# Interleaving the channels of a fused convolution and soft-MoE kernel, storing four evictions at a time, and giving the planner later landings

## The chip, the cores and the metric

The kernel runs on one core of a Trainium2 chip. The metric is the device time of one execution in microseconds, as the median of several runs; a run's time is a little longer than the span that the profiler draws from the first to the last instruction. The engines are named as in the profile: PE (matmul; PEld is its weight load), DVE (vector), ACT (scalar), POOL (GpSimd) and SP, which here only issues DMAs.

## The reference

The first half is a convolution whose seven taps are drawn anew for every token and head and go through a softmax; the second half is a soft mixture of experts over its output. Cut to what matters:

```python
B, S, D, H, K = 8, 3584, 192, 8, 7              # group = D // H = 24 channels per head
w = softmax(weight_gen, axis=-1)                # [B, S, H, K]
x_unf[b, s, k] = x_pad[b, s + k]                # the last 7 tokens
x = einsum('bshk,bskhg->bshg', w, x_unf).reshape(B * S, D)      # 28672 tokens

logits = x @ phi                                # [28672, 32]: 8 experts x 4 slots
d = softmax(logits, axis=0)                     # over the tokens, per slot
slot_in = d.T @ x                               # [32, 192]
slot_out[e] = relu(slot_in[e] @ w1[e]) @ w2[e]  # per expert, hidden width 1024
c = softmax(logits, axis=1)                     # over the slots, per token
out = c @ slot_out                              # [28672, 192]
```

Everything is float32.

## The kernel before

**Tiling.** Tokens are cut into blocks of T = 26 (with the six before them 32 rows), four blocks make a group, and there are 276 groups; two groups make a pair (138 pairs), four pairs a block of the loop, eight pairs a unit (17 units, and a last one of two pairs). One softmax chunk of taps serves eight groups, that is one block of the loop. `x` lies in `big` as block diagonal by head, so that one matmul with a 128x26 weight (four heads by 32 rows; `band`, the taps laid out as a band matrix) and 96 moving columns (four heads by 24 channels) gives the convolution of one block for four heads. A float32 matmul shows up as two MATMUL records in the trace.

**The stages.**

- *The loop.* For each pair, `conv` makes 16 matmuls into one PSUM bank (`cv`), four at a time in the four 32-row quadrants of the output, and ACT copies the 384 columns into `tm` (`conv_out`). In a pair's row of `tm` stand, between two ones, the 192 channels of the even group and the 192 of the odd group. `xpose` turns three pieces of 128 columns per pair by PE transposes, and ACT copies them into `cm`. The middle piece holds 64 channels of the even and 64 of the odd group; the odd group's halves are swapped, so that it ends with its first 96 channels.
- *Logits, per unit.* `logits` multiplies `cm` with `phi`: for each of the two groups of a pair and each of the two pieces that the group touches, four matmuls (one per quadrant) of 8 pairs x 26 = 208 columns. DVE takes the maximum (`top`, row L288, then L290), PE spreads it over the partitions (`newmax`, L306), DVE reduces it again (L310), ACT takes the exponential (L318), DVE transposes it (L327) and PE adds the tokens to the slots (`dispatch`, L346), two units being in flight.
- *The tail of the loop and the experts.* After the last rescale of the slot sums `accS` (L354), PE sums the even and odd groups' sums into slot inputs (`pst`, L704 to L706, and `psu`); the odd selector `selO4` and the zeros of `si` are made on POOL (L689, L690). Then come the expert matmuls (L742, L763).
- *The output.* For each of 16 steps of 17 or 18 groups, `rows` multiplies the transposed token weights `cT` with the slot outputs; ACT and DVE copy PSUM to `big` (`leave`, L823: an *eviction* of two PSUM banks), and SP stores it (`store`, L830). `out_order` lists 24 *items*; an item is four quarters of a step, in two evictions. The first item is stored in three parts, the second in two, every other whole. `big` is a ring of 16 eviction slots.

**What sets the order.** In the loop every step is an entry `op(engine, cost, reads, writes, function, ..., late=..)` of a list. PE's and SP's entries keep the list's order. For DVE, ACT and POOL a planner (`model`) plays the list with the costs given, a DMA's result being there `cost + late` after its issue begins, and lets each engine take the ready entry with the least slack; the sort by the times that it finds is the order in the program. On the chip every engine then works through its instructions strictly in that order, so a DVE instruction that waits for a DMA holds up all that stand behind it. The taps of a chunk are loaded by `loadw` (L160) and first read by `tap_top` (L171) on DVE; `tap_sub` (L175) follows on POOL, an exponential on ACT, a sum on POOL, a reciprocal on DVE (L194), a product on POOL (L202), and the transpose into the band on DVE (L206).

The two entries whose numbers matter:

```python
op(SP, 0.4, [], [("w", c % NTAP, b) for b in range(CH)], loadw, c, late=4.0)
op(SP, 2.0, [("z", i, h) for h in range(4)], [x_of(i)], loadx, i, late=3.0)
```

Of the kernel before, what the change touches and what calls it, by code (L numbers as in the profile page):

```python
# [8 lines left out]
F32 = mybir.dt.float32  # L9
# [41 lines left out]
def conv_soft_moe(ctx, tc, xh, wh, phi, w1a, w1b, w2, out):  # L51
# [169 lines left out]
    def conv(p):  # L221
        cv = cvs[p % NCV]
        for par in range(2):
            g = 2 * p + par
            t = g // SGG
            for c in range(2):
                for blk in range(4):
                    o = 4 * GW * (2 * par + (c ^ par))
                    i, b = ((4 * (g % m) + blk) * 2 + c for m in (4, SGG))
                    P.matmul(cv[32 * blk : 32 * blk + T, o : o + 4 * GW],  # L230
# [43 lines left out]
    def logits(u, lo=0, hi=UP):  # L274
        hi = min(hi, UNITS[u][1])
        cm = cms[u]
        lp = lss(u).rearrange("p (a b) j -> p a b j", b=2)
        for par in range(2):
            for i in range(2):
                for blk in range(4):  # L280
                    P.matmul(lp[32 * blk : 32 * blk + 32, lo:hi, par, 0:T],  # L281
                             phi_sb[:, 2 * par + i, :], cm[:, lo:hi, 1 if i else 2 * par, blk, :],
                             start=(i == 0), stop=(i == 1))
# [261 lines left out]
    for k in range(BLOCKS):  # L545
# [11 lines left out]
        for c in range(NTAP, NCH):  # L557
            if k == max(0, c - 4):
                op(SP, 0.4, [], [("w", c % NTAP, b) for b in range(CH)], loadw, c, late=4.0)
        for t in range(NSG):  # L560
            if (SGG * t + SGG - 1) // (2 * Q) == k:
                if t + NXS < NSG:
                    for i in (NXS - 1, NXS) if t == 0 else (t + NXS,):
                        op(SP, 2.0, [("z", i, h) for h in range(4)], [x_of(i)], loadx, i, late=3.0)
# [28 lines left out]
    op(PO, 0.3, [], tmf, drop, final)  # L593
    op(TE, 0.21 * FILL[0], [], [("cv", (PAIRS + 1) % NCV)], fill, FILL[0])
    op(TE, 0.19 * n, cm_of(final), [("ls", 1), spare], logits, final)
# [93 lines left out]
    G.tensor_tensor(out=selO4, in0=sel4, in1=selE4, op=ALU.subtract)  # L689
    G.memset(si, 0.0)  # L690
# [14 lines left out]
    P.matmul(pst[0:96], accS[:, 96:192], sO, start=False, stop=True)  # L705
    P.matmul(pst[96:128], accS[:, 0:32], sO, start=False, stop=True)  # L706
# [5 lines left out]
    for r in (0, 64):  # L712
        P.matmul(psu[r : r + 64], accS[:, 129 : D + 1], sE, start=True, stop=False)
        P.matmul(psu[r : r + 64], accS[:, 32:96], sO, start=False, stop=True)
# [121 lines left out]
    for kind, h, stores in out_order():  # L836
        for parts in stores:
            slot += -slot % len(parts)
            lo = at = slot % OT * 2 * 18 * T
            for qs in parts:  # L840
                po = ps_o.tile([128, 2, 512], F32, tag="po", name=f"po{kind}{h}_{qs[0]}")
                for i, q in enumerate(qs):
                    if kind == 0:
# [102 lines left out]
```

## Time and profile before

| | us |
|---|---|
| three runs | 307.57, 302.77, 307.64 |
| median of the runs | 307.57 |
| the profiled execution's own time | 305.91 |
| its span | 304.1 |
| first convolution matmul to the last rescale of the slot sums | 13.55 to 228.30 |
| experts, up to the first output matmul | to 244.52 |
| output: first store issued, last bytes moved | 246.23, 302 |

PE is busy for 263.5 us (87%) of the span, DVE for 197.2 (65%), ACT for 189.6 (62%), POOL for 146.6 (48%). These shares average over a loop in which PE hardly rests and an output stage in which the DMA engines do not, so they are read stage by stage. Lines marked L are lines of the kernel before; in the changed kernel most move by one.

### The profile page before, as it was taken

The page shows a single profiled execution, that of the slowest core. Times are in us where ns is not written, and L with a number is a line of the kernel's source. Part 1 is how long each engine was busy: PE and PEld are TensorE (multiplying, and loading weights), DVE is VectorE, ACT ScalarE, POOL GpSimd, SP SyncE. Part 2 cuts the span into 40 slices and gives each one's busy share as a digit, 9 for nine tenths or more (in the row PEclk, how much of TensorE's full clock was granted, in tenths as well). Part 3 has the DMA queues.
Part 4 walks back from the last instruction along what each step waited for, and adds up shares of the span by engine and source line. Part 5 has one row for each costly group of instructions (what it writes and reads, how often), then busy time and mean ns, then how long its engine had stood idle before and what let it go on. Part 6 is the DMA issues. An engine that isn't in the chain of part 4 may idle for free.

```text
span 304.1 us, 15222 instructions
## 1 busy us (share of the span) xinstructions
PE 263.5 (87%) x6646; PEld 213.7 (70%) x6646; DVE 197.2 (65%) x337; ACT 189.6 (62%) x399; POOL 146.6 (48%) x254
## 2 busy tenths in 40 slices
PE   8898998999999999999999999499899887889100
PEld 8787977888897888888988889488678632233000
DVE  8867757975787867775776855554056579995200
ACT  9896676576686767677767667255521268788400
POOL 8856556746468384665565463410017526550000
PEclk9999999999999999999999999979999999779855
DMA  6768676667677667666677666626748059999994
GB/s 184 220 180 240 201 214 199 208 205 207 185 216 202 201 187 202 195 194 193 185 222 216 188 204 195 195 81 182 255 130 314 3 202 416 421 410 417 419 418 204
DMA packets 26993, 69.24 MB, mean 228 GB/s; under 512 B 5936, under 2 KB 10800, under 8 KB 26928
## 3 DMA queue, kind: packets, MB, share of 16 engines
q1 hardware_dynamic: 26928, 68.28, 69.0%
q8 instruction: 52, 0.85, 1.2%
q14 instruction: 13, 0.11, 0.1%
HBM read 46.21 MB, written 22.04 MB: 224 GB/s over the span
## 4 chain that ended last, share of the span: by engine, by line
PE 69%; DMA 9%; DVE 7%; issue 4%; ACT 3%; POOL 3%; ACTq 1%; POOLq 0%; DVEq 0%
PE cv L230 30%; PE pt L250 14%; PE acb L346 7%; PE ls L281 7%; DMA out<-big 4%; DMA taps<-wh 4%; PE po L818 3%; PE so L763 2%; PE hpb L742 2%; PE acb L306 2%; DVE big L823 1%; DVE band L206 1%; POOL taps L175 1%; ACT big L823 1%; DVE cT L404 1%
## 5 line engine op out<-in xcount | busy, mean ns | idle before, releaser
L230 PE MATMUL cv<-big,band 128*26 128x96 f32 x4416 | 112.3, 250 | 3.6 <-issue 2.6
L230 PEld LDWEIGHTS cv<-big,band 128*26 128x26 f32 x4416 | 101.5, 130 | 13.0 <-issue 8.1
L236 ACT COPY tm<-cv 128x384 f32<-128x384 f32 x138 | 66.4, 482 | 57.6 <-PE cv L230 57.4
L206 DVE STREAM_TRANSPOSE band<-wide 128x1664 f32<-128x1664 f32 (+1 forms) x37 | 65.5, 1773 | 7.8 <-POOL wide L202 7.6
L250 PE MATMUL pt<-ident,tm 122*128 122x122 f32 x414 | 50.9, 272 | 0.2 <-issue 0.2
L257 ACT COPY cm<-pt 128x416 f32<-128x416 f32 x103 | 48.1, 511 | 1.9 <-PE pt L250 0.9
L250 PEld LDWEIGHTS pt<-ident,tm 122*128 122x128 f32 x414 | 44.5, 144 | 2.6 <-issue 0.4
L202 POOL TENSOR_TENSOR wide<-exps,sum 128x364 f32<-128x364 f32 (+1 forms) x36 | 28.5, 792 | 26.5 <-DVE sum L194 18.9
L175 POOL TENSOR_TENSOR taps<-taps,top 128x364 f32<-128x364 f32 (+1 forms) x36 | 28.5, 793 | 24.3 <-DVE top L171 24.0
L818 PE MATMUL po<-cT,so 32*128 32x442 f32 (+3 forms) x256 | 33.6, 629 | 5.4 <-ACT big L823 3.4
L823 ACT COPY big<-po 128x884 f32<-128x884 f32 (+2 forms) x33 | 28.1, 893 | 7.8 <-PE po L818 6.0
L818 PEld LDWEIGHTS po<-cT,so 32*128 32x128 f32 (+1 forms) x256 | 12.1, 171 | 26.4 <-ACT big L823 18.0
L188 POOL TENSOR_TENSOR si<-exps 128x208 f32<-128x208 f32 x32 | 20.3, 635 | 21.0 <-ACT exps L179 20.6
L281 PE MATMUL ls<-cm,phi_sb 128*32 128x208 f32 x544 | 28.9, 338 | 1.5 <-issue 1.5
L171 DVE TENSOR_REDUCE top<-taps 128x52 f32<-128x364 f32 (+1 forms) x37 | 17.7, 486 | 18.4 <-DMA taps<-wh 17.7
L346 PE MATMUL acb<-tm,dt 128*32 128x193 f32 x544 | 27.5, 328 | 2.3 <-issue 1.6
L87 POOL TENSOR_TENSOR LT<-LT,rm 128x544 f32<-128x544 f32 (+1 forms) x16 | 17.9, 1120 | 16.8 <-DVE rm L85 16.8
L288 DVE TENSOR_REDUCE mx<-ls 128x1 f32<-128x416 f32 x17 | 9.9, 584 | 24.0 <-PE ls L281 24.0
L281 PEld LDWEIGHTS ls<-cm,phi_sb 128*32 128x32 f32 x544 | 17.8, 109 | 6.9 <-issue 2.7
L346 PEld LDWEIGHTS acb<-tm,dt 128*32 128x32 f32 x544 | 18.0, 110 | 6.5 <-issue 3.1
L179 ACT ACTIVATE exps<-taps 128x364 f32<-128x364 f32 (+1 forms) x37 | 17.9, 493 | 6.3 <-POOL taps L175 6.3
L99 POOL TENSOR_TENSOR LT<-LT,sm 128x544 f32<-128x544 f32 (+1 forms) x16 | 17.9, 1121 | 6.8 <-DVE sm L97 6.6
(113 smaller groups left out, 260.1 us busy)
## 6 DMA issues: line engine op xcount, KB each, us to landing
big<-xh SPq DMA_DIRECT2D x276, 96.0 KB, 3.3
out<-big SPq DMA_DIRECT2D x18, 884.0 KB, 10.5
taps<-wh SPq DMA_DIRECT2D x34, 182.0 KB, 3.7
big<-w SPq DMA_DIRECT2D x8, 768.0 KB, 4.3
w1a_sb<-w1a SPq DMA_DIRECT2D x16, 256.0 KB, 3.6
out<-big SPq DMA_DIRECT2D x4, 936.0 KB, 4.9
w1b_sb<-w1b SPq DMA_DIRECT2D x8, 256.0 KB, 3.6
out<-big SPq DMA_DIRECT2D x3, 468.0 KB, 3.0
```

What stands on the lines that cost most here:

```text
L175: eng.tensor_tensor(out=t, in0=t, in1=each(tops.pop((c, b.start)), b.stop - b.start), op=ALU.subtract)
L188: eng.tensor_tensor(out=s, in0=t[:, :, :, 0:4], in1=t[:, :, :, 4:8], op=ALU.add)
L202: eng.tensor_tensor(out=dst, in0=exps[c % NEX][:, b, :, 0:KT], in1=each(m, n), op=ALU.mult)
L206: V.transpose(bands[c % NBAND][:, b].rearrange("p b j l -> p (b j l)"), wide[:, b].rearrange("p b j -> p (b j)"))
L230: P.matmul(cv[32 * blk : 32 * blk + T, o : o + 4 * GW], bands[g // 8 % NBAND][:, g // 4 % CH, :, i], xbd[:, place(t), :, b * GW : (b + 1) ...
L236: copy(tms[u % NTM][:, pr, 1 : 2 * D + 1], cvs[p % NCV][:, 0 : 2 * D])
L250: P.transpose(pt[:, at, 0:TR], tms[u % NTM][0:TR, pr, 1 + 128 * i : 129 + 128 * i], ident[0:TR, 0:TR])
L257: copy(cms[u].rearrange("p a i b j -> p (a i b) j")[:, at : at + n], pts.pop((k, j)).rearrange("p i (b j) -> p (i b) j", j=32)[:, 0:n, 0:T])
L281: P.matmul(lp[32 * blk : 32 * blk + 32, lo:hi, par, 0:T], phi_sb[:, 2 * par + i, :], cm[:, lo:hi, 1 if i else 2 * par, blk, :], start=(i = ...
L346: P.matmul(ac[32 * q : 32 * q + 32], dt[:, g, :], tm[:, g // 2, o : o + D + 1], start=(g < 4), stop=(g + 4 >= 2 * n))
L818: P.matmul(po[dst : dst + hi - lo, at, 0 : n * T], so[32 * q : 32 * q + 32, lo:hi], cT[32 * q : 32 * q + 32, g0 : g0 + n, 0:T], start=True ...
L823: (V.tensor_copy if done[1] % 3 == 1 else A.copy)(big[:, at : at + w].rearrange("p (q c) -> p q c", c=n * T), po[:, 0 : len(qs), 0 : n * T])
```

## The change

**Channels interleaved.** The 192 channels are renumbered as g * 8 + head in place of head * 24 + g. `conv` writes its 96 columns to PSUM no longer side by side but with a step of eight floats: four heads next to each other, 24 times. The odd groups' channels are rolled on the host, so that the odd group's last 128 columns are the same channels as the even group's first 128. The first and third transposed pieces of a pair then meet the same weights, and one logits matmul of 416 columns (8 pairs x 2 x 26) serves both; the middle piece keeps two matmuls of 208 columns. `phi`, `w1` and the selector step (`pst`: two matmuls for three) follow the new numbering.

**Two POOL steps moved into the list.** The zeros of `si` are written after the last use of `fold`, and `selO4` after the last logits, where both stood behind the last `mark` on POOL.

**Stores of four evictions.** From the fourth item on, two items (four evictions) share one store; the last stands alone. There are 17 stores in place of 27. The pending softmax steps of the output (`late`) are now handed out after each eviction in place of each store.

**Later landings.** In the list, a load of taps is given 0.45 + 5.2 us in place of 0.4 + 4.0, and a load of `x` 2.3 + 3.8 in place of 2.0 + 3.0.

```diff
@@ conv
             for c in range(2):
+                to = cv[:, D * par : D * par + D].rearrange("p (g e) -> p e g", e=H)[:, 4 * c : 4 * c + 4]
                 for blk in range(4):
-                    o = 4 * GW * (2 * par + (c ^ par))
                     i, b = ((4 * (g % m) + blk) * 2 + c for m in (4, SGG))
-                    P.matmul(cv[32 * blk : 32 * blk + T, o : o + 4 * GW],
+                    P.matmul(to[32 * blk : 32 * blk + T],
                              bands[g // 8 % NBAND][:, g // 4 % CH, :, i],
                              xbd[:, place(t), :, b * GW : (b + 1) * GW], start=True, stop=True)
@@ logits
+        for blk in range(4):
+            P.matmul(lp[32 * blk : 32 * blk + 32, lo:hi, :, 0:T], phi_sb[:, 0, :],
+                     cm[:, lo:hi, 0:3:2, blk, :], start=True, stop=False)
         for par in range(2):
-            for i in range(2):
-                for blk in range(4):
-                    P.matmul(lp[32 * blk : 32 * blk + 32, lo:hi, par, 0:T],
-                             phi_sb[:, 2 * par + i, :], cm[:, lo:hi, 1 if i else 2 * par, blk, :],
-                             start=(i == 0), stop=(i == 1))
+            for blk in range(4):
+                P.matmul(lp[32 * blk : 32 * blk + 32, lo:hi, par, 0:T], phi_sb[:, 1 + par, :],
+                         cm[:, lo:hi, 1, blk, :], start=False, stop=(par == 1))
@@ the list
-                op(SP, 0.4, [], [("w", c % NTAP, b) for b in range(CH)], loadw, c, late=4.0)
+                op(SP, 0.45, [], [("w", c % NTAP, b) for b in range(CH)], loadw, c, late=5.2)
...
+    op(PO, 0.45, ["fold"], ["si"], lambda: G.memset(si, 0.0))
...
+    op(PO, 0.5, ["sel4"], ["phi"], lambda: G.tensor_tensor(out=selO4, in0=sel4, in1=selE4, op=ALU.subtract))
...
-    G.tensor_tensor(out=selO4, in0=sel4, in1=selE4, op=ALU.subtract)
-    G.memset(si, 0.0)
@@ slot inputs
     P.matmul(pst, accS[:, 1:129], sE, start=True, stop=False)
-    P.matmul(pst[0:96], accS[:, 96:192], sO, start=False, stop=True)
-    P.matmul(pst[96:128], accS[:, 0:32], sO, start=False, stop=True)
+    P.matmul(pst, accS[:, 64:D], sO, start=False, stop=True)
@@ output
+    for store_of in out_order():
+        slot += -slot % len(store_of)
+        lo = at = slot % OT * 2 * 18 * T
+        for kind, h, qs in store_of:
...
+            at = leave(po, STEPS[h], qs, at)
             while late and late[0][0] < done[1]:
                 soft(pc, *late.pop(0)[1:])
+            if kind == 0 and qs[-1] == 3 and h + 4 < len(STEPS):
+                turn(h + 4)
+        store(lo, at)
+        slot += len(store_of)
@@ out_order
+    for p in parts[0] + parts[1]:
+        yield [p]
+    yield parts[2]
+    for i in range(3, len(parts), 2):
+        yield sum(parts[i : i + 2], [])
@@ host layout
+    odd = np.arange(SGG * 4) // 4 % 2 == 1
+    xg[:, odd] = np.roll(xg[:, odd], 8, axis=-1)
...
+    chan = np.arange(D).reshape(H, GW).T.reshape(D)
```

PE and SP keep their order in the loop. On DVE the new numbers move the readers of the taps. The first place is DVE in the fifteenth unit of the loop; `top` is the reader of a landed tap load, `mx` the unit's logits maximum, `nm` the spread maximum, `band` a finished band, `dt` the transposed exponentials. Before:

```order
L354 SCALAR_TENSOR_TENSOR accS<-accS,al_4126,acb 128x193
L171 TENSOR_REDUCE top_0_4166<-taps_84 128x52
L194 RECIPROCAL sum_0_4146<-sum_0_4146 128x52
L206 STREAM_TRANSPOSE band_92<-wide 128x1664
L288 TENSOR_REDUCE mx_4273<-ls 128x1
L290 TENSOR_SCALAR mq<-ls,mx_4273 128x4
L194 RECIPROCAL sum_0_4236<-sum_0_4236 128x52
L310 TENSOR_REDUCE nm_4289<-acb 128x1
L171 TENSOR_REDUCE top_0_4298<-taps_85 128x26
L327 STREAM_TRANSPOSE dt_4307<-dd 128x512
L294 STREAM_TRANSPOSE LT<-ls 128x512
```

And the same unit of the changed kernel:

```order
L355 SCALAR_TENSOR_TENSOR accS<-accS,al_4066,acb 128x193
L171 TENSOR_REDUCE top_0_4158<-taps_84 128x52
L289 TENSOR_REDUCE mx_4189<-ls 128x1
L291 TENSOR_SCALAR mq<-ls,mx_4189 128x4
L194 RECIPROCAL sum_0_4168<-sum_0_4168 128x52
L311 TENSOR_REDUCE nm_4226<-acb 128x1
L328 STREAM_TRANSPOSE dt_4241<-dd 128x512
L295 STREAM_TRANSPOSE LT<-ls 128x512
L206 STREAM_TRANSPOSE band_92<-wide 128x1664
L194 RECIPROCAL sum_0_4209<-sum_0_4209 128x52
L171 TENSOR_REDUCE top_0_4339<-taps_85 128x26
```

The reader of the taps still stands ahead of the unit's maximum, but the reciprocal and the band transpose no longer stand between the two; the next reader moved from ahead of `dt` to behind it.

The second place is DVE in the third unit, with the same names (`sm` is a sum of the token softmax). Before:

```order
L288 TENSOR_REDUCE mx_1064<-ls 128x1
L290 TENSOR_SCALAR mq<-ls,mx_1064 128x4
L93 TENSOR_REDUCE sm_1086<-LT 128x18
L310 TENSOR_REDUCE nm_1104<-acb 128x1
L194 RECIPROCAL sum_0_1060<-sum_0_1060 128x52
L171 TENSOR_REDUCE top_0_1118<-taps_85 128x52
L324 MEMSET dd 32x4
L327 STREAM_TRANSPOSE dt_1139<-dd 128x512
```

And of the changed kernel:

```order
L289 TENSOR_REDUCE mx_1045<-ls 128x1
L291 TENSOR_SCALAR mq<-ls,mx_1045 128x4
L171 TENSOR_REDUCE top_0_1069<-taps_84 128x52
L311 TENSOR_REDUCE nm_1079<-acb 128x1
L194 RECIPROCAL sum_0_1024<-sum_0_1024 128x52
L93 TENSOR_REDUCE sm_1089<-LT 128x18
L325 MEMSET dd 32x4
L328 STREAM_TRANSPOSE dt_1116<-dd 128x512
L206 STREAM_TRANSPOSE band_92<-wide 128x1664
L295 STREAM_TRANSPOSE LT<-ls 128x512
L171 TENSOR_REDUCE top_0_1184<-taps_85 128x52
```

The reader of `taps_85` moved from ahead of `dt` to behind `LT`, and that of the chunk before it (`taps_84`), which stood ahead of `mx`, now stands between `mq` and `nm`.

The third place is SP at the program's end, all the stores. Before:

```order
L415 DMA big<-w 128x1536 x8
L830 DMA out<-big 128x468 x2
L830 DMA out<-big 128x936 x3
L830 DMA out<-big 128x1872 x4
L830 DMA out<-big 128x1768 x18
```

And of the changed kernel:

```order
L416 DMA big<-w 128x1536 x8
L830 DMA out<-big 128x468 x2
L830 DMA out<-big 128x936 x3
L830 DMA out<-big 128x1872
L830 DMA out<-big 128x3744
L830 DMA out<-big 128x3640
L830 DMA out<-big 128x3536 x8
L830 DMA out<-big 128x1768
```

The first six stores stay as they were; then ten double stores and one single one take the place of 21.

More of the change, by code (lines that the diff above doesn't have):

```diff
@@ L563, in conv_soft_moe @@
                     for i in (NXS - 1, NXS) if t == 0 else (t + NXS,):
-                        op(SP, 2.0, [("z", i, h) for h in range(4)], [x_of(i)], loadx, i, late=3.0)
+                        op(SP, 2.3, [("z", i, h) for h in range(4)], [x_of(i)], loadx, i, late=3.8)
                     if t == 0:
@@ L593, in conv_soft_moe @@
     op(PO, 0.3, [], tmf, drop, final)
+    op(PO, 0.45, ["fold"], ["si"], lambda: G.memset(si, 0.0))
     op(TE, 0.21 * FILL[0], [], [("cv", (PAIRS + 1) % NCV)], fill, FILL[0])
[L595 removed]
+    op(TE, 0.19 * n, cm_of(final), [("ls", 1), spare, "phi"], logits, final)
+    op(PO, 0.5, ["sel4"], ["phi"], lambda: G.tensor_tensor(out=selO4, in0=sel4, in1=selE4, op=ALU.subtract))
     op(VE, 0.4, [], [("ls", 1), "mq"], top, final)
@@ L713, in conv_soft_moe @@
         P.matmul(psu[r : r + 64], accS[:, 129 : D + 1], sE, start=True, stop=False)
-        P.matmul(psu[r : r + 64], accS[:, 32:96], sO, start=False, stop=True)
+        P.matmul(psu[r : r + 64], accS[:, 0:64], sO, start=False, stop=True)
     for u in range(2):
@@ L876, in _unpack @@
     at = 0
-    for kind, h, stores in out_order():
-        n = STEPS[h]
-        for parts in stores:
-            qs = sum(parts, ())
-            w = 128 * len(qs) * n * T
-            a = flat[at : at + w].reshape(128, len(qs), n, T)
-            at += w
+    for store_of in out_order():
+        ws = [len(qs) * STEPS[h] * T for _, h, qs in store_of]
+        a = flat[at : at + 128 * sum(ws)].reshape(128, sum(ws))
+        at += a.size
+        for w, (kind, h, qs) in zip(ws, store_of):
+            n = STEPS[h]
+            b, a = a[:, 0:w].reshape(128, len(qs), n, T), a[:, w:]
             q = slice(qs[0], qs[-1] + 1)
@@ L886, in _unpack @@
             if kind == 0:
-                t[0:128, q, g] = a
+                t[0:128, q, g] = b
             else:
-                t[128:D, q, g] = a[0:64]
-                t[128:D, q, step(h + 1)[0] : sum(step(h + 1))] = a[64:128]
+                t[128:D, q, g] = b[0:64]
+                t[128:D, q, step(h + 1)[0] : sum(step(h + 1))] = b[64:128]
     t = t.transpose(2, 1, 3, 0).reshape(B, NB * T, D)
```

49 lines of the change are left out of this document (17 added, 32 removed).

## The prediction

> **What bounds the kernel now.** I read the strip of 40 slices (7.6 us each) first, then the windows by stage, then the waits, and the timeline where PE rested.
>
> ```profile
> PE   8898998999999999999999999499899887889100
> DMA  6768676667677667666677666626748059999994
> GB/s 184 220 180 240 201 214 199 208 205 207 185 216 202 201 187 202 195 194 193 185 222 216 188 204 195 195 81 182 255 130 314 3 202 416 421 410 417 419 418 204
> ```
>
> PE is the full row up to slice 30; in the last seven slices the DMA engines are full at some 418 GB/s, and PE falls back to 1 and 0. So the kernel has two bounds, one after the other, and each edit is priced in its own stage.
>
> ```profile
> 131.64:142.98 11.34, 11.34 (x351) 10.18 (x347) 8.31 (x14) 8.37 (x19) 5.86 (x10) 1.00 0.67 201
> 189.80:206.75 16.95, 13.14 (x363) 11.60 (x355) 9.48 (x15) 7.82 (x19) 4.75 (x9) 0.90 0.49 146
> ```
>
> The first row is the best unit of the loop: PE busy through all of 11.34 us. The second is the worst, 5.61 us longer, at a granted clock of 0.90. The timeline shows why (the first two rows are the same PE work in an undisturbed unit):
>
> ```profile
> 181.56 1.45 PE L250 MATMUL pt<-ident,tm 122*128 122x122 f32 x12
> 182.94 2.21 PE L230 MATMUL cv<-big,band 128*26 128x96 f32 x96
> 186.29 0.38 SPq L160 DMA_DIRECT2D taps<-wh  x1
> 191.21 1.50 PE L230 MATMUL cv<-big,band 128*26 128x96 f32 x64
> 191.49 0.54 DVE L171 TENSOR_REDUCE top<-taps 128x52 f32<-128x364 f32 x1 [4.48 <-DMA taps<-wh]
> 193.74 1.91 DVE L206 STREAM_TRANSPOSE band<-wide 128x1664 f32<-128x1664 f32 x1 [1.33 <-POOL wide L202]
> 195.57 0.55 DVE L288 TENSOR_REDUCE mx<-ls 128x1 f32<-128x416 f32 x1
> 196.16 0.22 DVE L290 TENSOR_SCALAR mq<-ls,mx 128x4 f32<-128x4 f32 x1
> 196.53 0.36 PE L306 MATMUL acb<-mq,sel 128*128 128x5 f32 x2 [3.81 <-DVE mq L290]
> 196.74 1.71 PE L250 MATMUL pt<-ident,tm 122*128 122x122 f32 x12
> 198.38 3.52 PE L230 MATMUL cv<-big,band 128*26 128x96 f32 x96
> ```
>
> DVE stood 4.48 us for taps whose load SP had issued only at 186.29, then made a reciprocal and a band, and only then the maximum that PE needed. PE stood 3.81 us, and ran slower afterwards.
>
> **Later landings: the fifteenth unit.** The load and its reader keep their places, so I let the taps land as before, and `top` run from 191.49 to 192.03. In the new order the maximum follows at once: 192.03, 0.59 later `mq` as in the rows, 0.22 for it and 0.15 to PE, which gives 192.99 in place of 196.53: **-3.5 us**. PE's convolution lasts to 192.71, so its wait shrinks to 0.3. What is late next is the band, which now stands behind `dt` and `LT`; its convolution belongs to a later half unit (5.7 us each), so it has room. Without the long rest I take back the slow stretch too: 3.52 - 2.21 and 1.71 - 1.45 make **-1.6 us**.
>
> **The third unit.**
>
> ```profile
> 51.02 0.53 DVE L171 TENSOR_REDUCE top<-taps 128x52 f32<-128x364 f32 x1 [1.99 <-DMA taps<-wh]
> 51.70 0.71 DVE L327 STREAM_TRANSPOSE dt<-dd 128x512 f32<-128x512 f32 x1
> 52.46 1.51 PE L346 MATMUL acb<-tm,dt 128*32 128x193 f32 x32 [0.60 <-DVE dt L327]
> ```
>
> The reader that held up `dt` moved behind it: **-0.6 us**. But readers have to stand somewhere. In the changed program the one before it stands between `mq` and `nm`, as one does in each of the next two units, and in seven units a reader stands directly ahead of the maximum. Behind a waiting reader are queued the maximum or its spread, then ACT's exponential, then PE's dispatch. This new exposure costs between nothing (if the taps have landed) and 3.8 us (another wait like the one above). I take the smaller wait that the trace shows, once: **+0.6 us**.
>
> **The tail of the loop.**
>
> ```profile
> 228.36 0.41 PE L704 MATMUL pst<-selE,accS 128*128 128x32 f32 x2
> 228.50 0.45 POOL L689 TENSOR_TENSOR phi_sb<-sel,selE 128x128 f32<-128x128 f32 x1
> 229.01 0.35 PE L705 MATMUL pst<-phi_sb,accS 128*96 128x32 f32 x2 [0.24 <-POOL phi_sb L689]
> 229.29 0.25 PE L706 MATMUL pst<-phi_sb,accS 128*32 128x32 f32 x2
> 229.47 0.32 PE L713 MATMUL psu<-selE,accS 128*64 128x32 f32 x4
> 229.61 0.29 PE L714 MATMUL psu<-phi_sb,accS 128*64 128x32 f32 x4
> 229.63 0.19 DVE L707 COPY si<-pst 128x32 f32<-128x32 f32 x1 [1.33 <-PE pst L706]
> ```
>
> With `selO4` ready, L705 follows L704 as L714 follows L713, 0.14 later: 228.50, ending at 228.85, and L706 is gone. The copy waited for L706's end (229.54); 229.54 - 228.85 = 0.69, of which I take **-0.6 us**. The zeros of `si` and `selO4` go into POOL's earlier idle time (POOL is busy for 5.86 of 11.34 us in the unit above); without that cover they would cost their 0.9 us again at most.
>
> **The logits.**
>
> ```profile
> 131.64 1.41 PE ls L281 x32
> 138.13 1.31 PE acb L346 x32
> 130.16 1.48 PE cv L230 x64
> ```
>
> Four quadrants run at once, so 32 records are eight steps: 1.41 / 8 = 176 ns for 208 columns, or 0.85 ns a column; the dispatch gives 1.31 / 8 / 193 = 0.85, the convolution 1.48 / 16 / 96 = 0.96. Time goes by columns, and these stay: 4 x 416 + 8 x 208 = 16 x 208. Saved are two of eight steps' fixed part, 96 x (0.96 - 0.85) = 11 ns each: 22 ns in 17 units, 0.4 us, or nothing. I take **-0.2 us**.
>
> **The strided PSUM write.**
>
> ```profile
> L230 PE MATMUL cv<-big,band 128*26 128x96 f32 x4416 | 112.3, 250 | 3.6 <-issue 2.6
> L230 PEld LDWEIGHTS cv<-big,band 128*26 128x26 f32 x4416 | 101.5, 130 | 13.0 <-issue 8.1
> L281 PEld LDWEIGHTS ls<-cm,phi_sb 128*32 128x32 f32 x544 | 17.8, 109 | 6.9 <-issue 2.7
> ```
>
> The trace before has no matmul that writes with a step between single columns. One bound: the logits already write runs of 26 with gaps, at the same 0.85 ns as the dispatch without gaps, so a break costs nothing. Other bound: the band's weight load reads columns a step of 32 floats apart, and 26 such take 130 ns where 32 adjacent ones take 109, at least 0.8 ns a column more. On the convolution's 4416 / 4 = 1104 steps of 96 columns that would be 85 us. I take nothing: a column comes only every 0.85 ns, a slow pace, and the logits' row is a write like this one, the weight load a read of another memory. The Trainium skill (PSUM — Partial Sum Buffer, Specifications (TRN2)) says the opposite: lines of 8 bytes, and any non-contiguous pattern slows matmuls significantly. By that sentence the sum would end on the slow side, in the second rival below; no row here shows it.
>
> **The output.**
>
> ```profile
> 246.23 0.82 SPq L830 DMA_DIRECT2D out<-big  x2
> 253.60 1.12 DVE L823 COPY big<-po 128x936 f32<-128x936 f32 x1
> ...
> 246.00:247.00 1.00, 1.00 (x10) 0.40 (x8) 0.95 (x2) 1.00 (x3) 0.28 (x1) 1.00 0.00 0
> 251.00:252.00 1.00, 0.47 (x8) 0.00 (x0) 1.00 (x2) 0.77 (x2) 1.00 (x2) 1.00 1.11 446
> 247.00:254.00 7.00, 5.43 (x50) 1.45 (x44) 6.37 (x10) 5.75 (x10) 2.41 (x3) 1.00 1.03 405
> 255.00:260.00 5.00, 3.99 (x30) 1.54 (x34) 4.91 (x8) 4.59 (x7) 3.28 (x3) 1.00 1.03 421
> out<-big SPq DMA_DIRECT2D x18, 884.0 KB, 10.5
> ```
>
> The first six stores hold 2 x 468 + 3 x 936 + 1872 columns of 128 x 4 bytes, 2.88 MB. By 254.0 the engines have moved 7 x 405 = 2.84 MB, so these are drained at 254.1. The seventh store now waits for two items; its last eviction is the DVE copy that ends at 254.72. From the first issue (246.23) to the first bytes went some 0.9 us (nothing moves before 247), so bytes flow again at 255.6, 1.5 us after the queue ran dry. On DVE a reciprocal now stands ahead of that copy, which makes up to 2.0; I take **+1.6 us**. It is not won back, since the engines are full from there to the end; PE and the evictions run ahead, and the last store is as small as before. The ten double stores carry 18.3 MB, 43.4 us at 421 GB/s. Larger pieces may move faster: at most at the best microsecond's 446, 40.9 us, which is -2.4; at least not at all. From the small early stores to the later ones the rate rose by 4%, part of it the start; I take a quarter of that, **-0.5 us**. The Trainium skill (DMA: Bandwidth & Descriptors, Measured) has 341 GB/s for 1 MB and 425 for 16 MB, so doubling should pay visibly; by it most of the 2.4 would come. The row of 421 at 0.9 MB a store speaks against it.
>
> **Sum.** -3.5 - 1.6 - 0.6 + 0.6 - 0.6 - 0.2 + 1.6 - 0.5 = -4.8. From the profiled execution's own 305.91 that is **301.1 us**. The runs before lie at 302.77 and twice at 307.6, with the profiled one between: against their median of 307.57 the forecast is 2.1% less, against the fastest run 0.6%. If that fastest run simply lacked the long wait, the change has little left to win over it.
>
> **Rivals.**
> - *The landing waits move on.* The 3.5 and 1.6 come back at one of the ten exposed readers. For it: 4.48 us of landing wait in one place, and the same SP order. Against: the list now allows for landings of over 5 us. The time is 301.1 + 5.1 = 306.2.
> - *The strided write costs, and the kernel is slower.* Place: the 1104 convolution steps, where PE is the bound. It decides from (307.57 x 1.02 - 301.1) / 1104 = 11 ns a step, 0.12 ns a column, over the slow mark; at the weight load's price the time is 301.1 + 85 = 386. For it the weight load, against it the logits.
> - *Large stores run at the best rate*: 301.1 - 1.9 = 299.2.
> - *The logits product does nothing for time.* That is in the sum already, at 0.2.
>
> **Chances.** Forecast, give or take 2.5 us: 0.50. Waits move on: 0.27. Fast stores: 0.11. Strided write: 0.10. The rest, 0.02, is a longer dry queue in the output. The range goes from 298 (fast stores and a little more) to 307.5 (waits move on, and the new exposure at twice its price); outside lie the strided write and the edges of the others. A measurement of this kernel tells about 2% from no change, 6.2 us. The forecast lies on that mark against the median, and well inside it against the fastest run, so half of it (0.25) and two thirds of the fast stores (0.07) count as faster: 0.32; slower is the strided write and the rest, 0.12; within, 0.56.
>
> **What would show it.** Right: no PE wait above 1 us on L290's row, and a loop from 13.5 to about 222; the L705 row 0.14 behind L704; a dry stretch of some 1.5 us in the DMA row after the sixth store; conv pieces of 64 records at 1.48 us still. Wrong: such pieces above 1.55, which is the strided write; a wait of PE on `mq` or `dt` of several us; or no dry stretch.

## The result and the profile after

| | before | after |
|---|---|---|
| median of 22 runs, us | 307.16 | 303.62 |
| lowest to highest, us | 302.77 to 312.04 | 301.42 to 308.04 |
| ratio, 95% interval | | 0.9947 [0.9921, 0.9972] |
| profiled execution, its span, us | 305.91, 304.1 | 308.04, 306.3 |

By the ratio the change gains half a per cent. That is clear of no change by its interval, but well inside the 2% from which a kernel is called faster here; 1.6% was forecast from the profiled execution (2.1% from the median). The ratio leaves out executions more than 1.5% above the fastest one of their kernel (10 of 22 before, 3 of 22 after) and so hangs on that one fastest execution, which is why medians of all runs of one chip stand beside it. The medians differ by 3.5 us, 1.2%.

The profiled execution of after is the longest of its 22. The strip of 40 slices (7.7 us each) shows one place in the loop, slice 12, where PE falls to 7 tenths and the granted clock to half:

```profile
PE   8989998999879898998999979999889987986600
PEclk9999999999959999999999999999999999599555
GB/s 187 219 156 212 177 218 194 190 197 224 185 235 170 208 165 208 166 208 208 170 208 190 209 208 172 195 147 208 224 182 274 40 174 357 424 415 424 427 425 240
```

A row of the windows gives a stretch, its length, the busy time of PE, PEld, DVE, ACT and POOL, the granted clock, the DMA share and GB/s. Here is an undisturbed unit and then the one with that place:

```profile
62.60:74.00 11.40, 10.78 (x298) 9.01 (x292) 7.94 (x15) 7.82 (x18) 6.24 (x12) 1.00 0.69 201
74.00:93.00 19.00, 15.96 (x414) 14.29 (x406) 11.88 (x18) 9.74 (x23) 11.05 (x18) 0.82 0.75 211
```

And the timeline of after in that unit, the sixth:

```profile
79.09 1.54 SPq L160 DMA_DIRECT2D taps<-wh  x1
82.88 0.53 DVE L171 TENSOR_REDUCE top<-taps 128x52 f32<-128x364 f32 x1 [3.70 <-DMA taps<-wh]
83.32 1.90 DVE L206 STREAM_TRANSPOSE band<-wide 128x1664 f32<-128x1664 f32 x1
85.15 0.55 DVE L289 TENSOR_REDUCE mx<-ls 128x1 f32<-128x416 f32 x1
85.74 0.22 DVE L291 TENSOR_SCALAR mq<-ls,mx 128x4 f32<-128x4 f32 x1
86.10 0.56 PE L307 MATMUL acb<-mq,sel 128*128 128x5 f32 x2 [3.04 <-DVE mq L291]
86.52 2.68 PE L250 MATMUL pt<-ident,tm 122*128 122x122 f32 x12
89.13 3.75 PE L230 MATMUL cv<-big,band 128*26 128x96 f32 x96
```

It is the picture of before's fifteenth unit in another place: DVE stands 3.70 us for taps, a band goes ahead of the maximum, PE stands 3.04 us and then runs slowly (2.68 and 3.75 us for pieces that take 1.45 and 2.21 in an undisturbed unit). In this execution the wait had not gone; it had moved. The fifteenth unit has none.

The tail of the loop in after:

```profile
230.68 0.42 DVE L355 SCALAR_TENSOR_TENSOR accS<-accS,al,cv 128x193 f32<-128x193 f32 x1 [0.32 <-PE cv L347]
231.15 0.41 PE L705 MATMUL pst<-selE,accS 128*128 128x32 f32 x2
231.40 0.39 PE L706 MATMUL pst<-phi_sb,accS 128*128 128x32 f32 x2
231.82 0.19 DVE L707 COPY si<-pst 128x32 f32<-128x32 f32 x1 [0.72 <-PE pst L706]
```

From the end of the last rescale (231.10) to the copy are 0.72 us, where before had 1.33 (228.30 to 229.63): 0.6 us saved, as forecast. The loop of this execution ends at 231.1, where the prediction had asked for about 222; in the two other profiles of the changed kernel it ends at 220.8 and 224.9.

The groups of PE in after:

```profile
L230 PE MATMUL cv<-big,band 128*26 128x96 f32 x4416 | 112.1, 250 | 7.7 <-issue 5.5 <-DVE band L206 1.1 <-DMA big<-xh 1.0
L279 PE MATMUL ls<-cm,phi_sb 128*32 128x416 f32 x136 | 15.9, 513 | 0.4 <-issue 0.4
L283 PE MATMUL ls<-cm,phi_sb 128*32 128x208 f32 x272 | 15.8, 338 | 0.0
```

The convolution writes with a step of eight floats and takes 112.1 us, 250 ns a record, where it took 112.3 and 250: no cost of the step shows. The logits of a unit stand in the chain as 0.70 us of L279 and 0.70 of L283, so 1.40 where before had 1.41.

The output of after by windows, the dry stretch and then the long middle:

```profile
255.00:256.00 1.00, 0.96 (x16) 0.15 (x8) 1.00 (x4) 0.73 (x2) 0.07 (x1) 1.00 0.95 386
256.00:257.00 1.00, 0.54 (x4) 0.30 (x4) 1.00 (x3) 0.41 (x1) 1.00 (x2) 1.00 0.37 150
257.00:258.00 1.00, 1.00 (x8) 0.30 (x4) 0.90 (x3) 0.93 (x2) 1.00 (x2) 1.00 0.44 187
258.00:259.00 1.00, 0.47 (x4) 0.30 (x4) 1.00 (x2) 1.00 (x2) 0.10 (x1) 1.00 0.74 314
259.00:260.00 1.00, 1.00 (x6) 0.33 (x4) 1.00 (x2) 1.00 (x3) 0.81 (x1) 0.83 1.16 479
265.00:300.00 35.00, 19.46 (x152) 5.84 (x144) 16.73 (x23) 18.85 (x26) 6.08 (x6) 0.74 1.01 425
```

Against 425 GB/s the five microseconds lack 39 + 275 + 238 + 111 - 54 = 609 GB/s, or 1.4 us: the dry stretch is there. The middle of before, also 35 us:

```profile
262.00:297.00 35.00, 19.75 (x152) 7.22 (x148) 17.48 (x24) 19.27 (x27) 6.67 (x7) 0.75 1.01 416
```

So the large stores run 2% faster, 18.3 MB in 43.1 us in place of 44.0. By these rows the rate wins back 0.9 of the 1.4 us. From the first store's issue to the end of the span both kernels take 57.9 us (304.1 - 246.2, 306.3 - 248.4).

### The profile page after: what moved, and what is told of

It reads as the page before. It is cut to its first block, busy times and chain, and to the rows that moved or that the text cites. A ratio compares the mean times of both kernels' runs of the same rounds, so it can differ in the third digit from the quotient of the medians.

```text
span 306.3 us, 14911 instructions
## 1 busy us (share of the span) xinstructions
PE 264.6 (86%) x6500; PEld 209.3 (68%) x6500; DVE 198.2 (65%) x337; ACT 190.2 (62%) x399; POOL 146.7 (48%) x254
## 4 chain that ended last, share of the span: by engine, by line
PE 63%; DMA 10%; DVE 9%; issue 7%; POOL 3%; ACT 2%; SPq 1%; ACTq 1%; POOLq 0%
PE cv L230 28%; PE pt L250 13%; PE acb L347 8%; DMA out<-big 5%; DMA big<-xh 3%; PE ls L279 3%; PE ls L283 3%; PE so L763 2%; PE hpb L742 2%; DVE big L823 2%; PE acb L307 2%; DVE cT L405 1%; DMA taps<-wh 1%; DVE band L206 1%; ACT big L823 1%
## 5 line engine op out<-in xcount | busy, mean ns | idle before, releaser
L230 PE MATMUL cv<-big,band 128*26 128x96 f32 x4416 | 112.1, 250 | 7.7 <-issue 5.5
L250 PE MATMUL pt<-ident,tm 122*128 122x122 f32 x414 | 51.8, 276 | 0.0
L250 PEld LDWEIGHTS pt<-ident,tm 122*128 122x128 f32 x414 | 45.5, 147 | 2.4
L818 PE MATMUL po<-cT,so 32*128 32x442 f32 (+3 forms) x256 | 35.4, 683 | 7.6 <-ACT big L823 4.7
L347 PEld LDWEIGHTS acb<-tm,dt 128*32 128x32 f32 x544 | 18.3, 110 | 5.2 <-issue 2.8
L194 DVE RECIPROCAL sum<-sum 128x52 f32<-128x52 f32 (+1 forms) x37 | 16.4, 444 | 7.0 <-POOL sum L190 6.8
L823 DVE COPY big<-po 128x884 f32<-128x884 f32 (+2 forms) x16 | 16.5, 1043 | 6.9 <-DMA out<-big 5.9
```

Of the source, the lines that this page charges most:

```text
L230: P.matmul(to[32 * blk : 32 * blk + T], bands[g // 8 % NBAND][:, g // 4 % CH, :, i], xbd[:, place(t), :, b * GW : (b + 1) * GW], start=Tru ...
L250: P.transpose(pt[:, at, 0:TR], tms[u % NTM][0:TR, pr, 1 + 128 * i : 129 + 128 * i], ident[0:TR, 0:TR])
L347: P.matmul(ac[32 * q : 32 * q + 32], dt[:, g, :], tm[:, g // 2, o : o + D + 1], start=(g < 4), stop=(g + 4 >= 2 * n))
L818: P.matmul(po[dst : dst + hi - lo, at, 0 : n * T], so[32 * q : 32 * q + 32, lo:hi], cT[32 * q : 32 * q + 32, g0 : g0 + n, 0:T], start=True ...
L823: (V.tensor_copy if done[1] % 3 == 1 else A.copy)(big[:, at : at + w].rearrange("p (q c) -> p q c", c=n * T), po[:, 0 : len(qs), 0 : n * T])
```

## The experiments

Each of the five sets of runs was made on one chip beside the kernel before; over the sets (three chips) its median lay between 305.05 and 307.85, so kernels are compared by their distance to it. Theory A is the prediction's: the landing waits sit at fixed places, which the new list clears. Theory B: each execution draws where a landing comes late.

### Each part alone

The part named is applied to the kernel before, as in the diff above. The two POOL steps alone:

```diff
+    op(PO, 0.45, ["fold"], ["si"], lambda: G.memset(si, 0.0))
+    op(PO, 0.5, ["sel4"], ["phi"], lambda: G.tensor_tensor(out=selO4, in0=sel4, in1=selE4, op=ALU.subtract))
-    G.tensor_tensor(out=selO4, in0=sel4, in1=selE4, op=ALU.subtract)
-    G.memset(si, 0.0)
```

> The kernel before with the later landings in the list and nothing else. Theory A (the prediction): the long wait for taps in the fifteenth unit is a fixed place of the program before; taking the band out from ahead of the maximum wins some 5 us, ratio 0.983 by medians. Theory B: a landing is late in one unit or another of every execution, the old order and the new are exposed to much the same degree, and the profile before showed one draw; then the list alone wins 0 to 2.5 us, ratio 0.992 to 1.000, and its profile shows a wait of PE for mq of 2 us or more in some other unit.

> The kernel before with stores of four evictions and nothing else. Theory A: a dry stretch of 1.5 us after the sixth store and 0.5 us won back by larger pieces, +1.1 us, ratio 1.004. Theory B: larger pieces win as much as the dry stretch costs, +-0.3 us, ratio 0.999 to 1.001; from the first store to the last byte it takes 55.7 us as before. Rival: stores alone win 1 us or more, ratio below 0.997.

> The kernel before with interleaved channels, the 416-column logits product and the two-matmul pst, and nothing else. Theory A: columns set the time, -0.2 us and up to 0.3 us in the tail; ratio 0.998 to 1.000; 64 convolution records in 1.48 us. Rival (strided write): slower, from 1.54 us for 64 records and 1.02 on. Theory C: fewer PE instructions leave fewer waits of the kind that the profile calls issue; then 1 to 2 us are won, ratio 0.994 to 0.997.

> The kernel before with the zeros of si and selO4 moved into the list, and nothing else. Theory A: the tail of the loop shortens by 0.4 to 0.6 us (the second selector matmul follows the first without a wait for POOL), ratio 0.998. Theory B: the planner's order in the loop changes as well, and what that does is as large: ratio between 0.994 and 1.004.

| alone (before: 305.05) | median, us | lowest to highest | ratio |
|---|---|---|---|
| later landings | 301.57 | 300.53 to 302.41 | 0.9915 [0.9882, 0.9949] |
| stores | 305.34 | 301.09 to 309.98 | 0.9985 [0.9938, 1.0032] |
| channels | 304.58 | 301.76 to 306.65 | 0.9989 [0.9954, 1.0025] |
| POOL steps | 304.21 | 299.88 to 307.70 | 0.9972 [0.9933, 1.0012] |

The list carries the gain: only its ratio has an interval that leaves out 1. Its 3.5 us by medians lie between the 5 of theory A and the 0 to 2.5 of theory B, and its profile has no wait on `mq` over 0.5 us, where B expected one of 2 us or more. The profiles of the other three have DVE's order in the loop unchanged, and yet none has before's wait of 3.8 us in the fifteenth unit; each has one of that size in the third. The profile with the channels alone, PE's timeline:

```profile
49.39 0.56 PE L307 MATMUL acb<-mq,sel 128*128 128x5 f32 x2 [3.77 <-DVE mq L291]
```

With the stores alone and with the POOL steps alone it is 3.73 and 3.53 us, at 49.5 and 50.8. So the one place that I priced was not fixed, against A; but three times in the third unit is no free draw, against B.

### The change whole, and with one part left out

```diff
-    yield parts[2]
-    for i in range(3, len(parts), 2):
+    for p in parts[2:7]:
+        yield p
+    for i in range(7, len(parts), 2):
```

This makes the doubling of the stores begin four items later (`after_late_doubles`). The others put back the stores of before, or the list's four numbers.

> The changed kernel itself, unaltered, so that it stands beside its parts on one chip. Theory 'sum' (the four parts act apart: later landings 0.9915, stores 0.9985, channels 0.9989, the two POOL operations 0.9972, product 0.986): 0.986 of before, some 300.8 us. Theory 'in company' (with the fewer, larger stores and the other channel order the new list is worth less than alone, because the landing that comes late is met at another place): 0.995 as first measured. In its profile, 'sum' expects no PE wait over 1 us on mq or on the band copy; 'in company' expects the 1.9 us wait of the sixth unit's top operations on tap landings to be there again.

> All of the change but the stores of four evictions: later landings, interleaved channels, the two POOL operations in the list; output in stores of two as before. If the stores are worth what they were alone (0.9985, interval 0.994 to 1.003), this runs at the changed kernel's ratio plus 0.15%, that is within half a per cent of it. If the dry stretch at the first double store (1.45 us in the profile) counts in full and the larger pieces' rate doesn't make it good, this is up to 1.4 us (0.5%) faster than the changed kernel.

> The changed kernel, but the doubling of the stores begins four items later, when the ring of evictions is ahead of the queue. If the dry stretch and the better rate of the large pieces offset each other (stores worth nothing in sum), this keeps the rate and loses the dry stretch: the output part some 1 to 1.5 us shorter, 0.3 to 0.5% under the changed kernel. If the rate of the last pieces is what limits, no change. In its profile the windows of the output's first 15 us show no stretch under 300 GB/s after the first stores.

> The changed kernel with the four numbers of the list (0.45, 5.2, 2.3, 3.8) put back to 0.4, 4.0, 2.0, 3.0: the landings are expected early again, all else is changed. Theory 'sum': the list is worth 0.9915 here as alone, so this runs 2.6 us over the changed kernel, near 0.9946 of before. Theory 'in company': the changed kernel's ratio within 0.3%. In its profile, a PE wait of 3 to 4 us on mq behind a tap landing in some one unit (third or fifteenth so far), and over 10 us of DVE's top operations waiting on DMA.

| (before: 305.07) | median, us | ratio of medians | ratio |
|---|---|---|---|
| changed kernel | 300.34 | 0.9845 | 0.9959 [0.9899, 1.0018] |
| without the stores | 300.37 | 0.9846 | 0.9935 [0.9886, 0.9984] |
| doubling later | 299.92 | 0.9831 | 0.9902 [0.9852, 0.9953] |
| with the old list | 303.53 | 0.9950 | 1.0024 [0.9959, 1.0089] |

In company the list is worth 303.53 - 300.34 = 3.2 us by medians, near what it is worth alone (3.5). All the rest is worth 1.5 us by the medians and nothing by the ratio. By the medians the parts add up, to about 4.5 us for 4.7 measured; by the ratios they do not, since the list alone (0.9915) gains more than the whole change (0.9959, with an interval that holds both). The stores are worth 0.0 us. With the doubling later, the dry stretch is gone, as its windows show:

```profile
247.00:248.00 1.00, 0.74 (x8) 0.00 (x0) 1.00 (x3) 0.50 (x1) 1.00 (x2) 1.00 0.99 397
248.00:249.00 1.00, 0.24 (x4) 0.21 (x8) 1.00 (x2) 0.99 (x2) 0.53 (x1) 1.00 1.11 457
...
250.00:251.00 1.00, 0.50 (x6) 0.30 (x4) 1.00 (x2) 0.50 (x1) 0.97 (x1) 1.00 0.95 397
251.00:252.00 1.00, 1.00 (x8) 0.30 (x4) 0.90 (x3) 0.84 (x2) 1.00 (x2) 0.78 1.10 449
...
259.00:294.00 35.00, 17.30 (x152) 5.87 (x144) 16.82 (x23) 18.91 (x26) 6.16 (x6) 0.83 1.01 426
```

No microsecond is near the 150 of after, and the rate of the middle stays. The output part takes 56.6 us in place of 57.9; the median fell by only 0.4 us (0.14%), where 0.3 to 0.5% was expected. The dry stretch is thus a real price, which the better rate had in part paid for. In the loop, this profile has the sixth unit's wait again:

```profile
86.07 0.36 PE L307 MATMUL acb<-mq,sel 128*128 128x5 f32 x2 [3.52 <-DVE mq L291]
```

In the changed kernel's second profile (298.31 us) that same wait is 0.43 us, at 83.06. The place is the same, the size differs from one execution to the next.

### Which of the list's numbers, and how far

```diff
-  op(SP, 0.45, ..., loadw, c, late=5.2)          # the change: taps 0.45, 5.2
-  op(SP, 2.3, ..., loadx, i, late=3.8)           #             x 2.3, 3.8
+  later_list:      taps 0.45, 6.6     x 2.3, 4.6
+  earlier_list:    taps 0.4, 2.8      x 2.0, 2.2
+  new_taps_old_x:  taps 0.45, 5.2     x 2.0, 3.0
+  old_taps_new_x:  taps 0.4, 4.0      x 2.3, 3.8
```

In the expectations t, B and MX with a number are DVE's `top` of a chunk, its band copy and a unit's `mx`, counted from 0: MX5 is the maximum of the sixth unit.

> The changed kernel with its landings in the list later still (taps 6.6 instead of 5.2 us, x 4.6 instead of 3.8). In the list of the change the column maximum of the sixth unit (MX5) stands behind two top operations at once (t16, t17), and two of its five profiles so far wait there for 3.0 and 3.5 us; in this list MX5 stands behind one (t16, then the band copy). Theory 'place' (a landing that is late costs PE only where two readers stand ahead of a column maximum): the wait of the sixth unit is gone, the profile shows no PE wait over 1 us on mq or the band copy but perhaps in the ninth (t22, t23 ahead of MX8); median 0 to 1 us under the changed kernel, highest run under 302. Rival 'too late' (readers put off leave the bands late, and PE waits for DVE's band copy instead): PE's waits on the band copy, 1.1 us now, grow past 3 us, and the time by 2 us and more over the changed kernel.

> The changed kernel with its landings in the list earlier than before the change (taps 0.4 and 2.8, x 2.0 and 2.2). Theory 'place': more top operations stand ahead of a column maximum with their taps not landed, so DVE's top operations wait over 17 us in all, PE waits 3 to 4 us on mq in two or more units, the median is 2 to 6 us over the old list's 303.5, so 305 to 310, and single runs spread by over 8 us. Rival 'draws without places' (what the list orders makes no difference but by chance): within 1.5 us of the old list's kernel.

> The changed kernel with the x loads' numbers put back (2.0 and 3.0) and only the tap loads later (0.45, 5.2). The waits in the profiles come by tap landings, and only 0.5 us at a time by x landings: theory 'taps' gives this the whole gain of the list, 0.3 us within the changed kernel, so some 3 us under the old list's kernel. MX5 stands behind t16 and t17 here too, so the wait of the sixth unit can occur. Rival 'x': half the gain or less.

> The changed kernel with the tap loads' numbers put back (0.4 and 4.0) and only the x loads later (2.3, 3.8). Here the column maximum of the third unit no longer stands behind t10 and t11 (it does in the old list, and five of five profiles of the old list wait there or in the fifteenth unit), but MX5 stands behind t15, t16 and t17 in one stretch. Theory 'taps': 1.5 us or more over the changed kernel, as the old list's. Theory 'place': no wait in the third unit, one of over 3 us in the sixth, and a time between the two kernels, 301 to 303.

| (before: 307.19) | median, us | ratio of medians | ratio |
|---|---|---|---|
| later still | 302.75 | 0.9855 | 0.9932 [0.9880, 0.9984] |
| earlier | 307.65 | 1.0015 | 1.0062 [1.0007, 1.0117] |
| taps alone later | 304.39 | 0.9909 | 0.9922 [0.9869, 0.9974] |
| x alone later | 300.89 | 0.9795 | 0.9847 [0.9779, 0.9914] |

My theory 'taps' fell: the x numbers give the larger part, though the waits are on taps. A list that allows the landings less time (earlier) is level with before within 1%, but its profile has one large wait, not the two or more that were expected. PE's timeline with the earlier list, then with the taps alone later:

```profile
51.77 0.56 PE L307 MATMUL acb<-mq,sel 128*128 128x5 f32 x2 [5.56 <-DVE mq L291]
```

```profile
62.32 0.36 PE L307 MATMUL acb<-mq,sel 128*128 128x5 f32 x2 [3.08 <-DVE mq L291]
```

With x alone later the profile has 0.6 us of waits on `mq` in all, and not the wait of over 3 us in the sixth unit that 'place' expected. With the later list none is above 0.2, but its highest run is 308.13, not under 302. The rival 'too late' is seen there only in part: waits on the band copy doubled, from 1.1 to 2.2 us. The largest waits in its profiled execution (306.77 us) are of another kind, the group "issue", which is idle time of PE for which the profile shows no cause. A row gives the us in total, how many times, and the longest:

```profile
PE cv L230 <- issue: 9.3, 13, 1.6
PE cv L230 <- DVE band L206: 2.2, 3, 0.8
PE acb L347 <- issue: 1.5, 2, 1.1
```

### On one chip, and list and stores together

`after_third` is the changed kernel, `x_again` the list with x alone later, `old_list_again` the old list; `x_late_doubles` has x alone later and the doubling later.

> The changed kernel, unaltered, beside the next three. Theory 'pairs' (what counts is how many top operations stand ahead of one column maximum; the change leaves t16 and t17 ahead of MX5, and t22, t23 ahead of MX8): 1.2 to 1.6% under before in medians, 2.5 to 3.5 us under the old list's kernel. Its profile shows the sixth unit's wait of 3 us or none.

> Again the changed kernel with only the x loads' numbers later (2.3, 3.8), the tap loads' at 0.4 and 4.0. If the x numbers carry the gain (the last call: 0.985 of before in fast runs, 0.9795 in medians), it runs level with the changed kernel within 1 us or under it, and 2.5 us or more under the old list's. If the last call's number was a matter of six runs (one of them at 306.4), it falls halfway, 1 to 2 us over the changed kernel. In its profile 'pairs' expects no wait in the third unit, since only t10 stands ahead of MX2, and at most one of 3 us in the sixth (t15, t16, t17 ahead of MX5).

> The changed kernel with the old list, as base of this call: 0.99 to 1.00 of before in medians, highest runs above 305, and in the profile a PE wait of 3 to 4 us on mq in the third unit (t10 and t11 ahead of MX2) or in the fifteenth.

> The x-only list with the doubling of the stores four items later. If list and stores add up: 0.4 to 1.2 us under the run with the x-only list, since the dry stretch of 1.45 us goes and the rate of the last eight stores stays; the windows of the output's first 15 us show no microsecond under 300 GB/s after the second. If the stores make no difference at all: within 0.4 us of it.

| (before: 307.83) | median, us | ratio of medians | ratio |
|---|---|---|---|
| changed kernel | 302.48 | 0.9826 | 0.9824 [0.9759, 0.9890] |
| x alone later | 302.30 | 0.9820 | 0.9846 [0.9795, 0.9897] |
| old list | 306.16 | 0.9946 | 0.9997 [0.9950, 1.0044] |
| x alone later, doubling later | 301.25 | 0.9787 | 0.9801 [0.9746, 0.9857] |

The x numbers alone do as well as all four. The list is worth 306.16 - 302.48 = 3.7 us here. The old list's wait is there again, 4.20 us at 50.55. The doubling four items later gives 1.0 us more (the output part 57.1 in place of 58.1 us), as expected.

### Moving the step, and taking it away

Why do tap waits answer to x numbers? Both only matter through the order. In DVE's order I counted the tap readers ahead of each unit's `mx`, less two for every unit before it (a unit uses up two chunks):

```
unit                 1 2 3 4 5 6 7 8 9 ...
old list             7 7 8 8 8 8 8 8 8      waits of 3.5 to 4.2 us: third unit (5 of 6 profiles)
earlier              7 7 8 8 8 8 8 8 8      5.6 us: third
taps alone later     7 7 7 8 8 8 8 7 8      3.1 us: fourth
the change           7 7 7 7 7 8 8 8 8      3.0 and 3.5 us: sixth (2 of 6), else 0.6 or less
x alone later        7 7 7 7 7 8 8 8 8      none over 1.8 us (3 profiles)
later still          7 7 7 7 7 7 7 7 8      none
```

Where the count steps from 7 to 8, one reader goes ahead of the maximum a unit earlier than those before it, while SP's order has its load no earlier. Wherever these profiles have a wait of 3 us or more, it is in the first such unit, but for before's in the fifteenth. The reverse does not hold: the change has its step in every profile and the wait in two of six, x alone has the step and in three profiles no wait there, and the later list's step in the ninth unit and the second one of the taps alone cost nothing.

The rows of SP say what is late there. In the nine of these profiles with the wait at a step, DVE begins to stand between 1.7 us before and 0.2 us after SP issues the load, and the reader runs 2.7 to 4.6 us after that issue, where a tap load of before takes 3.7 in the median. So these landings are not unusually long; the reader comes too early for its load's issue. Only in before's fifteenth unit is the landing itself long, 5.2 us. This also suggests why the x numbers count. In the planner SP takes its loads in order, so a dearer load of `x` moves the planned issue of the tap load behind it, and with it the reader. That is read from the planner's code; no run parts the two numbers of an x load.

Two last runs test the step, with the change's other parts kept:

```diff
-  old list:    loadw, c, late=4.0
+  one_load:    loadw, c, late=5.0 if c == 9 else 4.0     # step in the fourth unit
+  even_list:   taps 0.45, 8.0   x 2.3, 5.5, doubling later   # no step, 7 in every unit
```

> The changed kernel with the old list, but for one load: the taps of chunk 9 are given 5.0 us to land in place of 4.0. In DVE's order this moves the step from 7 to 8 top operations ahead of the column maximum from the third unit (t11 ahead of MX2) to the fourth (t13 ahead of MX3). Theory 'step' (the reader that first steps one further ahead meets a load issued at its old time, and the first such unit pays): no wait in the third unit at 49 to 51 us, a wait of 2 to 4 us on mq at 60 to 63 us, and a time near the old list's, 0.99 to 1.00 of before in medians. Rival 'size' (what helps is that all landings are allowed more time): the third unit's wait stays, since the other loads keep their 4.0.

> The changed kernel with the doubling of the stores four items later and the list's landings far later (taps 8.0, x 5.5), by which 7 top operations stand ahead of every column maximum and no unit has a step. Theory 'step': no PE wait on mq over 0.6 us anywhere in the loop, loop's end as early as in the best profiles so far, no execution above 303 on the slower chip, 0.975 to 0.985 of before in medians. Rival 'too late': the bands come late, PE's waits on the band copy rise from 1.1 us to over 3 us, and the time is 2 us or more over the changed kernel's.

| (before: 307.85) | median, us | ratio of medians | ratio |
|---|---|---|---|
| one load later | 308.31 | 1.0015 | 1.0043 [0.9998, 1.0088] |
| no step | 299.46 | 0.9727 | 0.9773 [0.9698, 0.9848] |

With one load's number changed, the timeline has the wait in the fourth unit, and the third has 0.2 us:

```profile
55.48 0.35 SPq L160 DMA_DIRECT2D taps<-wh  x1
59.22 0.53 DVE L171 TENSOR_REDUCE top<-taps 128x52 f32<-128x364 f32 x1 [5.43 <-DMA taps<-wh]
62.91 0.55 DVE L289 TENSOR_REDUCE mx<-ls 128x1 f32<-128x416 f32 x1
63.86 0.56 PE L307 MATMUL acb<-mq,sel 128*128 128x5 f32 x2 [3.43 <-DVE mq L291]
```

Without a step, PE's waits in the loop (us in total, times, longest) are:

```profile
PE cv L230 <- issue: 3.3, 4, 1.7
PE acb L347 <- issue: 3.0, 3, 1.5
PE cv L230 <- DVE band L206: 1.9, 3, 0.8
PE acb L307 <- DVE mq L291: 0.8, 2, 0.5
```

'Step' foretold the unit (60 to 63 us, found at 63.9) and the size of the wait, 3.4 us; the load is again issued after DVE began to stand (55.48, 53.79). It missed on the time with one load later (1.0015 by medians, where 0.99 to 1.00 was expected) and on the loop of the kernel without a step, which ends at 224.0 and so not as early as in the best profile (220.8, on another chip). 'Too late' fell: the waits on the bands are 1.9 us in place of the changed kernel's 1.1, and not over 3. The kernel without a step lies further below its before (8.4 us) than the changed kernel in any set (3.5 to 5.3), but its interval, 0.970 to 0.985, still holds 2%. The two did not run in one set, and the later doubling is in it too: x alone later with that doubling, which has a step, lies 6.6 us below its before. That the missing step gives the rest is argued, not shown.

## Why the prediction was off

**Later landings (-3.5 - 1.6 - 0.6 + 0.6 = -5.1): the step that failed.** The mechanism was right, a tap reader that waits ahead of the maximum; the size was off: the list is worth 3.2 to 3.7 us by medians of all runs, alone and in company (by the ratios 0.65 to 1.7%, or 2.0 to 5.3 us). I took the wait of one execution as a fixed property of the order. Of the six profiles with the old list, only that of before has its large wait in the fifteenth unit; the five others have theirs in the third. The prediction had the doubt itself (a fastest run that "simply lacked the long wait"), but the sum stayed with the one execution. And I took it that the new list has no such place. It has one, in the sixth unit, which cost 3.0 and 3.5 us in two of six profiles and 0.6 or less in four. My rival "the landing waits move on" (306.2 us, 0.27) had the mechanism, in a third of these profiles. Two thirds of -5.1 would be -3.4, near what was measured; but six profiles are few, and x alone later has the same step and no such wait, so that reckoning is not shown. The upper end of the range does not come out of its own words either: 306.2 with the new exposure at twice its price is 306.8, not 307.5.

**The reference.** The sum was made from the profiled execution, 305.91, which lay 1.3 us under the median of 22 runs; that is half of the 2.5 us between 301.1 and 303.62. Its -4.8 us stand against -3.5 by the medians of the first measurement and -4.7 and -5.3 in two later sets; by the ratio of the first it is 0.53% of 307 us, or -1.6. Where the total came near, that was luck: the list gave 1.4 to 1.9 us less than forecast, and all the rest 1.5 and 1.7 us of gain where the sum had a loss of 0.3.

**The new exposure (+0.6)** was sought directly ahead of the maximum, in seven units. Where the new list did wait 3 us, it was in one unit, the one in which the count of readers steps up. That can be counted in the order alone, but I looked only at places where before had waited.

**The tail (-0.6)** is right in the rows, 0.61 us; the second selector matmul starts 0.25 us behind the first, not 0.14. **The logits (-0.2)**: 1.40 in place of 1.41 us a unit, so next to nothing, as the rival had it. **The strided PSUM write (0)**: right. That rival, 0.10 at 386 us, is out: records at 250 ns before and after.

**The output (+1.6 - 0.5 = +1.1)**: 0.0 measured, 57.9 us both. The dry stretch was 1.4 us; the rate rose by 2%, where I had taken 1%. The rows leave 0.5 us of loss that the whole part does not show; it was not traced. "Large stores at best rate" went too far, since 425 GB/s are under the 446 of the best microsecond. The Trainium skill (DMA: Bandwidth & Descriptors, Measured) was right in direction, a larger transfer moves faster. Its table is of loads issued from GpSimd, 341 GB/s at 1 MB and 425 at 16 MB. That is a quarter more for four doublings, where the stores here gave 2% for one, 416 to 425 GB/s from 0.9 to 1.8 MB.

**Open.** All that is not the list gives 1.5 and 1.7 us by medians where rows account for 0.6, and by the ratio nothing. Why before's own profile paid in the fifteenth unit and not at its step isn't settled either, nor why a step costs PE 3 us in one execution and nothing in another.

## What to carry to other kernels

One profile shows one draw: before pricing a wait at full size, ask whether another execution of the same order would have it, and compare the run-to-run spread with the wait. In an order that a planner writes, count how far ahead the readers of loads stand at each milestone, and look where that count steps, since that unit may pay even if all later ones run clean; ask too when the load is issued, not only how long it takes to land. A list whose count never steps took 2.7% off by medians (with the later doubling), the numbers of the change 1.2 to 1.7%, and x alone later with that doubling 2.1%, on other chips. Where a larger transfer starves a queue at its start, begin with small ones until the producer is ahead: here that kept the rate without the gap.

## What the hardware showed beside this

A matmul that writes PSUM with a step of 32 bytes between columns ran at the speed of one that writes them side by side. The sentence of the Trainium skill (PSUM — Partial Sum Buffer, Specifications (TRN2)), that any non-contiguous pattern slows matmuls significantly, did not hold for this float32 convolution (250 ns a record in both).

PE's idle time of the kind "issue", for which the profile shows no cause, came to between 3.5 and 11.0 us in the loop of one execution, and did not fall with fewer instructions (5.9 us in before; 4.5, 7.9 and 8.8 in the three profiles of the change). In the chain that ended last, as the changed kernel's second profile has it, four of its five pieces of over 0.6 us in the loop lie at nearly even distances:

```profile
99.20 1.13 issue
...
135.37 0.91 issue
...
170.94 0.80 issue
...
205.92 0.61 issue
```

The distances are 36.2, 35.6 and 35.0 us. The fifth piece (0.71 us at 45.47) does not fit them, and other profiles have pieces between, so the regularity is not shown to be general. What causes this idle time no run here tells; in the kernel without a step it is the largest that is left in the loop.
